# Pooled attention and a ReLU² feed-forward on one core: the exchange of q's halves on GpSimd or VectorE instead of by DMA

## The chip, the cores and the metric

The kernel runs on one core of a Trainium2 chip. The metric is the device time of one execution in microseconds; the kernel before was run three times. The core's engines are TensorE (PE; its weight loads are listed as PEld), VectorE (DVE), ScalarE (ACT), GpSimd (POOL) and SyncE (SP), which here only issues DMAs.

## The reference

Attention over four batches of eight heads, with the queries averaged in pairs, and then a feed-forward with a squared ReLU on the heads laid side by side:

```python
# q, k, v: (4, 8, 1152, 64) f32; w_in: (512, 2048); w_out: (2048, 512)
q_pool = q.reshape(B, H, S // 2, 2, D).mean(axis=3)          # 576 queries a head
scores = np.matmul(q_pool, k.transpose(0, 1, 3, 2)) / np.sqrt(D)
scores = scores - np.max(scores, axis=-1, keepdims=True)
attn = np.exp(scores)
attn = attn / (np.sum(attn, axis=-1, keepdims=True) + 1e-09)
x = np.matmul(attn, v)                     # -> (2304, 512) after a transpose
h = np.maximum(x @ w_in, 0.0)
out = (h * h) @ w_out
```

## The kernel before

**Tiling.** The 32 heads are worked through as 16 pairs of two heads. A pair has nine chunks of 128 queries by 1152 keys, so there are 144 chunks. Eight of them are of one head, and one holds the last 64 queries of both. Operands of matmuls are pairs of fp16 numbers, a high and a low part, whose products are added up; pairs 0 to 3 keep some operands in f32.

**A pair's preparation** (`prep(n)`, n is the number of the pair). SP loads k, q and v (LK, LQ, LV or LF). The two queries of a pair are added (QS, L486). A scale is found with a small matmul or sums of squares (GR, GM or QK, QQ, QV, then GF, GS, GE). q is scaled and split into a high and a low part (QA, L343 or L345; QD, L374), and so is k (KA, KD). A transposing DMA turns each of them: QT (L646) writes tile `qT`, KT (L633) writes tile `kT`. QT puts the high part of q on 64 partitions and the low part on the other 64. The low plane `qT[:, 1]` needs the halves the other way round, so step QX (two instructions, z = 0 and 1) copies each half of `qT[:, 0]` to the other 64 partitions. For pairs 1 to 4 (`'QXD': (1, 2, 3, 4)`) QX is a DMA from SBUF to SBUF, issued by SP at L652; for pairs 5 to 15 it is a copy on VectorE or GpSimd at L655. Pair 0 (`'FS': (0,)`) works in f32 and has no QX. A chunk's scores S wait for KT and both QX of their pair.

**A chunk.** S (L760, or L755 for the shared chunk), the maximum on VectorE (MX, L771), its bias (MB, L778 or L781), the exponential on ScalarE (EX, L795). For pairs 0 to 3 TensorE turns the result (TP, L836) and VectorE or ScalarE copies it to tile `PT` (TC, L846 and L848); for the other pairs it is split in two fp16 parts (HI, L799; LO, L807) and turned by a DMA (TR, L810). Two groups of matmuls per pair multiply with v (PV, L947 or L955).

**The feed-forward.** The result is worked on in nine blocks of 256 tokens (`block`). A block's columns are normalized (RV, RT, RB, XR: L1006 to L1046), scaled and split (XQ to XD), then there are eight steps of the hidden layer (H, L1119; HA, G1, G2, G3 square the ReLU) and eight of the output (O, L1168). Before that both weight matrices are loaded in sixteen parts (L1222) and turned into fp16 pairs (lines 1230 to 1347).

**The order.** Each operation is entered with `plan.add`: a name, the engines that may do it with a cost for each, what it depends on, and a position (`at`). `Plan.order` then simulates the engines, slots of buffers and a clock of TensorE, and writes out one program per engine. Among the operations that can start on an engine within its slack (`slPE` to `slSP`) it takes the one with the lowest priority number, which is the position plus an offset of the kind of operation (tables `off` and `off0`; `off0` counts up to the first block). An operation that may run on two engines goes to the one that can start it sooner, unless the other would end it earlier by more than `pen`. In the model a GpSimd operation waits for VectorE operations of the kinds in `LOCK`, QX among them, and these for it. Engines run their programs in order, so an instruction that waits holds all behind it.

The lines around the change:

```python
        def qx(o, z):
            t = qT(n).rearrange("p l c m -> p l (c m)")
            a, b_ = 64 * z, 64 - 64 * z
            if o["eng"] == "SP":
                nc.sync.dma_start(out=t[a : a + 64, 1], in_=t[b_ : b_ + 64, 0])
            else:
                e = nc.vector if o["eng"] == "DVE" else nc.gpsimd
                e.tensor_copy(t[a : a + 64, 1], t[b_ : b_ + 64, 0])
...
                add(("QX", n, z), {"SP": 850} if n in cfg("QXD", ()) else alt("QX", DVE=470, POOL=1500), [("QT", n)] + old, lambda o, z=z: qx(o, z), need)
```

## Time and profile before

| | before |
|---|---|
| median of 3 runs | 796.21 us (793.77 to 802.07) |
| profiled execution | 796.25 us |
| its span, first to last instruction | 794.4 us |
| TensorE busy | 743.8 us (94%) |
| VectorE busy | 571.4 us (72%) |
| ScalarE busy | 589.7 us (74%) |
| GpSimd busy | 350.1 us (44%) |
| chain that ended last: PE, DVE, ACT, DMA | 78%, 7%, 5%, 5% |

The busy shares are means over stages that differ: up to about 200 us the weights are prepared and pairs 0 to 4 begun; then scores, PV and the feed-forward share TensorE; from about 645 us on only the feed-forward is left. A wait of an engine is listed with what ended it. Idle time of an engine matters only where others wait for what it does next.

### The profile page before, as it was taken

How to read it: one execution, taken by the hardware profiler on the slowest of the kernel's cores; microseconds unless marked ns; L12 is line 12 of the kernel's file. 1: busy time of each engine (PE TensorE's matmuls, PEld its weight loads, DVE VectorE, ACT ScalarE, POOL GpSimd, SP SyncE). 2: the span in 40 equal slices, each digit the busy share in tenths (PEclk: the TensorE clock that was granted, in tenths of full speed). 3: DMA queues.
4: the chain of work that ended last, by engine and by line, in shares of the span. 5: the costliest groups of instructions: out<-in, count | busy, mean ns of one | idle time of the engine just before them, and what ended most of it. 6: DMA issues, size and time to landing. Idle time of an engine off the chain costs nothing.

```text
span 794.4 us, 15338 instructions
## 1 busy us (share of the span) xinstructions
PE 743.8 (94%) x5998; PEld 491.7 (62%) x5998; DVE 571.4 (72%) x920; ACT 589.7 (74%) x874; POOL 350.1 (44%) x240
## 2 busy tenths in 40 slices
PE   5889888888999999979999999999999999999997
PEld 4665555555766676546756775577567657785654
DVE  4789987787789798787879888898898764202311
ACT  5776967899798798688987997899989864403512
POOL 2455421346686475544646575575366321001200
PEclk8899899999899999979999999999999999999999
DMA  8686573417889999999999999999999991000011
GB/s 325 225 233 187 167 204 106 120 31 142 168 172 199 194 225 218 219 206 215 186 212 199 217 208 207 202 228 195 209 217 191 173 183 25 1 2 13 14 27 28
DMA packets 324840, 128.96 MB, mean 162 GB/s; under 512 B 307104, under 2 KB 307872, under 8 KB 324768
## 3 DMA queue, kind: packets, MB, share of 16 engines
q1 hardware_dynamic: 324768, 127.98, 77.3%
q8 instruction: 47, 0.77, 0.4%
q14 instruction: 25, 0.20, 0.1%
HBM read 45.09 MB, written 4.72 MB: 63 GB/s over the span
## 4 chain that ended last, share of the span: by engine, by line
PE 78%; DVE 7%; ACT 5%; DMA 5%; issue 3%; SPq 1%; POOL 0%; DVEq 0%; ACTq 0%; POOLq 0%
PE ba L1168 17%; PE ba L1119 17%; PE s L760 12%; PE ba L955 10%; PE bt L1168 7%; PE bt L1119 6%; DVE s L771 3%; PE ba L836 3%; DMA region<-in_moe_w_in_dram 2%; PE ba L947 2%; ACT buf L795 2%; PE s L755 2%; DMA w<-in_moe_w_out_dram 2%; DVE PT L848 1%; ACT PT L846 1%
## 5 line engine op out<-in xcount | busy, mean ns | idle before, releaser
L771 DVE TENSOR_SCALAR_CACHE_REDUCE s<-s,esc 128x1152 f32<-128x1152 f32 x135 | 190.9, 1420 | 32.2 <-PE s L760 21.9
L1119 PEld LDWEIGHTS <-w 128*128 128x128 f16 x1728 | 169.4, 99 | 33.1 <-issue 7.0
L795 ACT ACTIVATE buf<-s,ca 128x1152 f32<-128x1152 f32 x144 | 174.4, 1212 | 14.2 <-DVE s L771 7.7
L807 POOL TENSOR_TENSOR buf<-buf,buf 128x1152 f16<-128x1152 f32 x53 | 130.9, 2472 | 54.1 <-ACT buf L799 44.2
L760 PE MATMUL s<-kT,qT 128*128 128x512 f16 x720 | 137.6, 330 | 9.3 <-ACT buf L795 9.0
L1168 PE MATMUL ba<-w,region 128*128 128x512 f16 x624 | 142.2, 379 | 1.3 <-ACT region L1129 0.7
L1168 PEld LDWEIGHTS <-region 128*128 128x128 f16 x864 | 82.8, 98 | 96.3 <-issue 2.5
L1119 PE MATMUL ba<-region,w 128*128 128x256 f16 x1104 | 128.7, 275 | 1.3 <-DVE x L1046 1.2
L799 ACT ACTIVATE buf<-buf 128x1152 f16<-128x1152 f32 x107 | 124.5, 1163 | 5.9 <-DMA PT<-buf 1.7
L760 PEld LDWEIGHTS <-qT 128*128 128x128 f16 x720 | 63.6, 100 | 66.9 <-issue 18.1
L807 DVE TENSOR_TENSOR buf<-buf,buf 128x1152 f16<-128x1152 f32 x55 | 77.1, 1404 | 14.4 <-ACT buf L799 14.1
L955 PE MATMUL ba<-PT,v 128*64 128x320 f16 (+1 forms) x1296 | 85.4, 290 | 0.0
L955 PEld LDWEIGHTS <-v 128*64 128x64 f16 x1296 | 70.8, 111 | 14.7 <-issue 7.1
L1146 POOL TENSOR_TENSOR region<-region 128x512 f16<-128x512 f32 x35 | 49.2, 1405 | 51.4 <-ACT region L1139 50.0
L1146 DVE TENSOR_TENSOR region<-region 128x512 f16<-128x512 f32 x37 | 29.1, 793 | 58.7 <-ACT region L1139 55.8
L836 PE MATMUL ba<-ident,buf 128*128 128x128 f32 x324 | 54.4, 296 | 14.8 <-ACT buf L795 5.5
L1134 ACT ACTIVATE region<-region 128x512 f16<-128x512 f32 x72 | 45.1, 626 | 20.3 <-PE bt L1168 17.3
L836 PEld LDWEIGHTS ba<-ident,buf 128*128 128x128 f32 x324 | 36.4, 148 | 30.7 <-ACT PT L846 8.7
L1168 PE MATMUL bt<-w,region 128*128 128x512 f16 x240 | 52.6, 379 | 0.0
L1142 POOL TENSOR_TENSOR region<-region 128x512 f32<-128x512 f32 x11 | 14.6, 1329 | 83.6 <-ACT region L1134 83.6
L846 ACT ACTIVATE PT<-ba 128x384 f32<-128x384 f32 x76 | 35.7, 490 | 18.6 <-PE ba L836 17.1
L1119 PE MATMUL bt<-region,w 128*128 128x256 f16 x432 | 48.7, 273 | 0.0
(189 smaller groups left out, 944.1 us busy)
## 6 DMA issues: line engine op xcount, KB each, us to landing
raw<-in_q_dram SPq DMA_DIRECT2D x32, 288.0 KB, 3.8
raw<-in_k_dram SPq DMA_DIRECT2D x15, 576.0 KB, 4.8
region<-in_moe_w_in_dram SPq DMA_DIRECT2D x8, 1024.0 KB, 6.2
w<-in_moe_w_out_dram SPq DMA_DIRECT2D x8, 1024.0 KB, 5.8
raw<-in_v_dram SPq DMA_DIRECT2D x12, 576.0 KB, 4.7
out_dram<-buf SPq DMA_DIRECT2D x22, 128.0 KB, 2.4
v<-in_v_dram SPq DMA_DIRECT2D x4, 576.0 KB, 6.2
out_dram<-half SPq DMA_DIRECT2D x14, 128.0 KB, 3.3
```

Source lines behind the costliest of these rows:

```text
L760: nc.tensor.matmul(s[:, x, :w], lhsT=qt[:, l].rearrange("p c m -> p (c m)")[:, 128 * c0 + h : 128 * c0 + h + 255 : 2], rhs=rhs, **st)
L771: nc.vector.tensor_scalar(st3(), st3(), sc, 3e38, op0=ALU.mult, op1=ALU.min, accum_out=a[:, x : x + 1])
L795: nc.scalar.activation(P(), st3(), AF.Exp, bias=a[:, 1:2], scale=s1, accum_out=col)
L799: nc.scalar.activation(hl()[:, 0], P(), AF.Copy)
L807: e.tensor_tensor(out=hl()[:, 1], in0=P(), in1=hl()[:, 0], op=ALU.subtract)
L836: nc.tensor.matmul(t[:, y], lhsT=P()[:, c * 128 : (c + 1) * 128], rhs=ident, is_transpose=True, start=(y == 0), stop=(y == 2), skip_group_ ...
L846: nc.scalar.activation(out, t, AF.Copy)
L955: nc.tensor.matmul(px[h * 64 : (h + 1) * 64, 64 * r * (1 - h) : 64 * r * (1 - h) + N], lhsT=vv[:, h, kc, vl, :], rhs=p2(vi, r, h, 9 * pl + ...
L1119: nc.tensor.matmul(ph[:, f2], lhsT=w16[0][:, SLOT[f // 4], wl, a, f % 4 * 128 : (f % 4 + 1) * 128], rhs=xhl()[:, xl, a], start=(i == 0), s ...
L1134: nc.scalar.activation(gt[u][:, 0], rt[u % 2], AF.Square)
L1146: e.tensor_tensor(out=gt[u][:, 1], in0=rt[u % 2], in1=gt[u][:, 0], op=ALU.subtract)
L1168: nc.tensor.matmul(p[:, :DM], lhsT=g[:, gl, f % 2, tt * 128 : (tt + 1) * 128], rhs=w16[1][:, SLOT[f // 4], wl, f % 4], start=(f == 0 and g ...
```

## The change

`QXD` becomes empty, so the two QX of pairs 1 to 4 are no longer entered for SP but for VectorE or GpSimd, as those of pairs 5 to 15 are. All the numbers that steer the planner (positions of the weights, slacks, penalty and both tables of offsets, over two hundred in all) are replaced by others. No line of code differs otherwise. The diff, cut to single entries of the one line:

```diff
-CFG = {'SPLIT': 0, 'TURN': [], 'TURNB': [],
...
-'WSP': 0.4394, 'WOF': 23.2581, 'MSP': 10.7319, 'pen': 4650.4498, 'bl': 16.0216, 'slPE': 66.7964, 'slACT': 353.0356, 'slDVE': 0.0, 'slPOOL': 569.0059, 'slSP': 247.8544, 'off': {'ED': 1246.3547, 'EX': 5849.5041, 'G1': -389.0426,
...
-'PART': 1, 'QXD': (1, 2, 3, 4), 'MSC': (0, 1, 2, 3, 4, 5, 6, 7, 8, 9, 10, 11, 12, 13, 14, 15), 'FS': (0,), 'NSG': (12, 13, 14, 15)}
+CFG = {'SPLIT': 0, 'TURN': [], 'TURNB': [],
...
+'WSP': 0.0186, 'WOF': 22.3361, 'MSP': 10.3534, 'pen': 6673.337, 'bl': 12.9223, 'slPE': 128.2463, 'slACT': 204.4283, 'slDVE': 0.0, 'slPOOL': 713.7895, 'slSP': 699.821, 'off': {'ED': 1155.7513, 'EX': 5204.1755, 'G1': -68.3962,
...
+'PART': 1, 'QXD': (), 'MSC': (0, 1, 2, 3, 4, 5, 6, 7, 8, 9, 10, 11, 12, 13, 14, 15), 'FS': (0,), 'NSG': (12, 13, 14, 15)}
```

## Rows read from the trace of the kernel before

**Rows 1.** The page's head, and span and granted clock of the core.
```profile
span 794.4 us, 15338 instructions
...
core 0: 794.4 us, clock 0.973
```

**Rows 2.** Busy time by stretch: length, engines (instructions), granted clock, DMA share, GB/s.
```profile
0.00:199.30 199.30, 163.49 (x1261) 108.49 (x1262) 157.25 (x265) 156.79 (x235) 82.85 (x57) 0.95 0.60 174
199.30:340.00 140.70, 139.68 (x1153) 90.85 (x1154) 114.96 (x173) 115.49 (x171) 88.29 (x58) 0.98 1.05 198
340.00:366.00 26.00, 19.10 (x157) 11.47 (x153) 22.70 (x47) 22.62 (x33) 13.78 (x10) 0.79 1.09 217
366.00:645.00 279.00, 276.79 (x2369) 185.19 (x2369) 239.22 (x368) 244.10 (x359) 152.56 (x105) 0.99 1.08 203
645.00:794.40 149.40, 144.77 (x1072) 95.72 (x1066) 37.23 (x72) 50.66 (x80) 12.65 (x11) 0.99 0.13 28
```

**Rows 3.** TensorE around 350 us: start, length, operation, [idle before]; first a chain row.
```profile
313.21 3.79 PE ba L955 x54
...
341.04 1.14 PE L760 MATMUL s<-kT,qT 128*128 128x512 f16 x6 [0.82 <-ACT buf L795]
...
346.33 2.08 PE L760 MATMUL s<-kT,qT 128*128 128x512 f16 x6 [2.26 <-ACT buf L795]
...
350.18 2.08 PE L760 MATMUL s<-kT,qT 128*128 128x512 f16 x6 [1.55 <-ACT buf L795]
352.18 5.30 PE L955 MATMUL ba<-PT,v 128*64 128x320 f16 x54
...
359.38 2.78 PE L1119 MATMUL ba<-region,w 128*128 128x256 f16 x24
...
365.41 4.43 PE L1119 MATMUL ba<-region,w 128*128 128x256 f16 x24 [1.16 <-DVE x L1046]
```

**Rows 4.** End of the head: timeline, a chain row, and the stretch after it.
```profile
196.75 0.46 DVE L655 COPY qT<-qT 64x1152 f16<-64x1152 f16 x1 [2.12 <-DMA qT<-half]
...
199.31 2.08 PE L1119 MATMUL ba<-buf,w 128*128 128x256 f16 x9 [3.68 <-DVE region L1046]
...
199.31 5.28 PE ba L1119 x24
...
200.00:210.00 10.00, 10.00 (x69) 6.87 (x68) 6.19 (x10) 5.72 (x9) 5.33 (x5) 0.75 0.75 141
```

**Rows 5.** The exchange: DMAs by line (page), copies by line (busy, mean, idle before).
```profile
qT<-qT SPq DMA_DIRECT2D x8, 144.0 KB, 3.5
...
L655 POOL COPY qT<-qT 64x1152 f16<-64x1152 f16 x10 | 13.8, 1380 | 9.6 <-DMA qT<-half 7.1 <-DMA qT<-buf 2.2
...
L655 DVE COPY qT<-qT 64x1152 f16<-64x1152 f16 x12 | 12.1, 1005 | 3.5 <-DMA qT<-half 3.0 <-DMA qT<-buf 0.3
```

**Rows 6.** Timeline of SP's queue in the head, for pairs 1 and 3.
```profile
39.84 0.51 SPq L455 DMA_DIRECT2D raw<-in_k_dram  x1
42.23 1.16 SPq L652 DMA_DIRECT2D qT<-qT  x2
43.56 1.08 SPq L1222 DMA_DIRECT2D region<-in_moe_w_in_dram  x1
46.01 4.01 SPq L633 DMA_TRANSPOSE kT<-buf  x1
...
109.28 3.43 SPq L633 DMA_TRANSPOSE kT<-buf  x1
...
114.03 0.60 SPq L652 DMA_DIRECT2D qT<-qT  x1
```

**Rows 7.** Busy time from 110 to 120 us, columns as in rows 2.
```profile
110.00:120.00 10.00, 9.74 (x75) 6.04 (x72) 7.09 (x8) 6.32 (x14) 1.16 (x1) 1.00 0.97 261
```

**Rows 8.** Timeline of a pair's two copies, one on each engine.
```profile
356.06 1.21 POOL L655 COPY qT<-qT 64x1152 f16<-64x1152 f16 x1 [1.01 <-DMA qT<-buf]
356.30 1.28 DVE L655 COPY qT<-qT 64x1152 f16<-64x1152 f16 x1
```

More of the change, by code (lines that the diff above doesn't have):

```diff
@@ new lines @@
+CFG = {'SPLIT': 0, 'TURN': [], 'TURNB': [], 'WDP': ((1, 0), (1, 1), (1, 2), (1, 3)), 'WSP': 0.0186, 'WOF': 22.3361, 'MSP': 10.3534, 'pen': 6673.337, 'bl': 12.9223, 'slPE': 128.2463, 'slACT': 204.4283, 'slDVE': 0.0, 'slPOOL': 713.7895, 'slSP': 699.821, 'off': {'ED': 1155.7513, 'EX': 5204.1755, 'G1': -68.3962, 'G2': -123.9467, 'G3': 1333.2622, 'GE': 18.1176, 'GF': 26.104, 'GM': -745.2473, 'GR': -643.0342, 'GS': -84.6219, 'H': 954.7454, 'HA': -215.368, 'HI': -1269.3528, 'KA': 562.9266, 'KC': -57.49, 'KD': 497.1086, 'KT': -1299.5505, 'KX': 67.3497, 'LF': 35.8519, 'LK': -857.6213, 'LO': 760.731, 'LQ': 549.3415, 'LV': -11.1892, 'MB': -424.817, 'MX': 361.3027, 'O': 953.3253, 'OD': -275.6397, 'PV': 500.3755, 'QA': -1401.4099, 'QC': 29.2001, 'QD': 32.489, 'QK': 2138.8964, 'QQ': 146.18, 'QS': 2497.0738, 'QT': 1494.0203, 'QV': -11.834, 'QX': 1525.4262, 'QY': -276.7502, 'RB': 0.0, 'RT': 278.7151, 'RU': -195.812, 'RV': 249.435, 'S': 495.01, 'ST': 0.0, 'TC': -2615.772, 'TP': 409.8394, 'TR': 2599.4919, 'U0': -78.5472, 'U1': -57.609, 'U2': -4.104, 'U4': 39.0922, 'U5': -146.3559, 'UA': -84.0042, 'UB': 78.0938, 'UD': -134.7562, 'UG': 504.7818, 'UL': -415.8558, 'UM': 15.5013, 'US1': -635.3331, 'US2': -517.841, 'US3': -91.4049, 'VA': -109.6182, 'VD': -3.4512, 'W0': -284.5234, 'W1': -316.9133, 'W2': 2307.5158, 'W4': -13.01, 'W5': -32.0465, 'WA': -3.098, 'WD': 5824.783, 'WG': 373.7026, 'WL': 182.5255, 'WM': 231.0511, 'WS1': -78.0917, 'WS2': -2611.7598, 'WS3': 331.8007, 'XA': -778.7032, 'XD': -370.2665, 'XM': -210.263, 'XN': 63.9693, 'XO': 48.8333, 'XQ': 1.593, 'XR': -15.1029, 'XT': -199.6854, 'XU': -5.4353, 'XW': 57.8313, 'aG1': 215.9286, 'aG2': 181.1135, 'aG3': 3322.7748, 'aH': 524.2489, 'aHA': 315.5924, 'aO': 548.5746, 'aOD': -78.9785, 'aRB': 188.0562, 'aRT': 150.485, 'aRU': 36.8139, 'aRV': 455.1187, 'aST': -2.8218, 'aXA': 251.4545, 'aXD': 160.2636, 'aXM': 404.5088, 'aXN': -6.8193, 'aXO': 43.6287, 'aXQ': -286.9806, 'aXR': -104.2157, 'aXT': 0.0, 'aXU': -51.4745, 'aXW': 238.9049, 'zG1': -127.2733, 'zG2': 237.7114, 'zG3': 125.1926, 'zH': 62.4838, 'zHA': -114.0457, 'zO': -12.4775, 'zOD': -322.5224, 'zRB': 167.2084, 'zRT': 6.4244, 'zRU': -30.3756, 'zRV': 5.0063, 'zST': -706.033, 'zXA': 414.6013, 'zXD': 22.9561, 'zXM': -101.8686, 'zXN': -73.9566, 'zXO': 125.3875, 'zXQ': 1.9865, 'zXR': 314.746, 'zXT': -68.6324, 'zXU': 223.2691, 'zXW': -84.2701}, 'off0': {'ED': -320.0915, 'EX': 125.5949, 'G1': 248.867, 'G2': 110.9041, 'G3': -16.9689, 'GE': -47.3991, 'GF': -53.7139, 'GM': 404.5614, 'GR': 81.4246, 'GS': 386.4081, 'H': -53.165, 'HA': 321.1861, 'HI': 454.0458, 'KA': -73.3824, 'KC': 383.1779, 'KD': 32.3608, 'KT': -14.5959, 'KX': -109.4637, 'LF': -115.1952, 'LK': 283.9355, 'LO': -37.2674, 'LQ': -668.8801, 'LV': -6.9267, 'MB': 83.388, 'MX': 27.5904, 'O': -118.3342, 'OD': 608.16, 'PV': 109.2794, 'QA': 337.6865, 'QC': 336.4052, 'QD': -124.9362, 'QK': -273.3459, 'QQ': 129.9256, 'QS': 10.539, 'QT': -2000.7354, 'QV': 114.5733, 'QX': -194.2563, 'QY': -172.2764, 'RB': 96.2895, 'RT': 50.1838, 'RV': -16.9469, 'S': 0.6736, 'ST': -48.0614, 'TC': -136.814, 'TP': -1846.3967, 'TR': -590.0095, 'U0': 241.215, 'U1': 9.5267, 'U2': -333.3012, 'U4': 1.3978, 'U5': 166.1059, 'UA': 1.0166, 'UB': -165.2871, 'UD': -135.0975, 'UG': -341.5448, 'UL': -13.3372, 'UM': 163.4304, 'US1': 256.4171, 'US2': 1.0301, 'US3': 134.9024, 'VA': 140.927, 'VD': 568.9883, 'W0': 47.9826, 'W1': -423.8488, 'W2': 728.494, 'W4': -214.2481, 'W5': -106.9897, 'WA': -30.786, 'WD': -532.7241, 'WG': 117.0441, 'WL': -781.7529, 'WM': -460.7912, 'WS1': -0.4311, 'WS2': 84.5956, 'WS3': 173.9561, 'XA': 388.3773, 'XD': -123.6278, 'XM': 48.4282, 'XN': 62.3395, 'XO': -494.8718, 'XQ': -3.2534, 'XR': -12.8004, 'XT': 759.0058, 'XU': -0.293, 'XW': -0.2008, 'aG1': -470.7793, 'aG2': -105.6588, 'aG3': 379.2232, 'aH': 126.9171, 'aHA': 41.6135, 'aO': -179.083, 'aOD': -89.0891, 'aRB': 123.2573, 'aRT': -105.3376, 'aRU': 21.553, 'aRV': -75.9354, 'aST': -191.3426, 'aXA': -351.4751, 'aXD': -15.2288, 'aXM': -78.308, 'aXN': 382.8232, 'aXO': 10.5251, 'aXQ': 157.1809, 'aXR': 281.7874, 'aXT': -36.7704, 'aXU': 47.4239, 'aXW': -81.0074, 'zG1': -128.2889, 'zG2': 74.8859, 'zG3': -216.8134, 'zH': -687.1117, 'zHA': -13.0965, 'zO': 66.0008, 'zOD': 215.2758, 'zRB': -42.5762, 'zRT': -457.4963, 'zRU': -93.7426, 'zRV': -220.5694, 'zST': 3.3173, 'zXA': -48.9854, 'zXM': -20.2671, 'zXN': -180.6047, 'zXO': -90.0309, 'zXQ': 122.8555, 'zXR': -296.7451, 'zXT': -122.7678, 'zXU': 4.0233, 'zXW': -206.5981}, 'FV': (0, 1, 2, 3), 'PART': 1, 'QXD': (), 'MSC': (0, 1, 2, 3, 4, 5, 6, 7, 8, 9, 10, 11, 12, 13, 14, 15), 'FS': (0,), 'NSG': (12, 13, 14, 15)}
```

1 line of the change is left out of this document (removed).

## The prediction

> **What bounds the kernel now.** I first read the granted clock and the span, then the busy time by stretch, then the chain of waits, and last the timelines of the places that the change touches. The profiled execution took 796.25 us, of which 794.4 us are its span [rows 1]; the other 1.85 us lie around it. The median of the runs shown is 796.21 us, so the sums below, made against 796.25 us, can be read against the median as they stand.
>
> The table of stretches [rows 2] divides the span by what TensorE did. From 199.3 us on, TensorE is full: idle for 1.0 us of 140.7, 2.2 us of 279.0 and 4.6 us of the last 149.4. In these stretches the end moves only with TensorE's own work, and the change adds or removes no matmul. TensorE idles in two places. In the head (0 to 199.3 us) it idles 199.3 - 163.5 = 35.8 us in many small pieces, while VectorE is busy 157.3 us and ScalarE 156.8 us, each 79%; GpSimd is busy only 82.9 us and the DMA engines 60%. The head is a mesh of weight preparation and the first four pairs, in which no engine is full but VectorE and ScalarE are nearest to it. Between 340 and 366 us TensorE idles 26.0 - 19.1 = 6.9 us and its clock is 0.79 of the full rate: it had used up the feed-forward work of the blocks that were ready, and had only scores to do, each waiting for ScalarE's exponentials [rows 3]. So the span is TensorE's work plus about 50 us of idle time, 43 of them in those two places.
>
> The second place cost more than its idle time. After the gaps the clock fell from the upper level (2.4 GHz) to the lower (1.2 GHz): six score matmuls took 2.08 us twice in place of 1.14, a PV group of 54 matmuls 5.30 in place of 3.79, and 24 matmuls of a hidden layer 4.43 in place of 2.78 [rows 3]. That is 0.94 + 0.94 + 1.51 + 1.65 = 5.0 us, and with the idle time 11.9 us for one such stall. A smaller one ends the head: TensorE stands 3.68 us until 199.31, and its next 24 matmuls of the hidden layer, in a stretch with a clock of 0.75, take 5.28 us in place of 2.78 [rows 3, 4], so 3.7 + 2.5 = 6.2 us.
>
> **The change, part by part.** *Taken away:* eight DMAs of 144 KB, two for each of pairs 1 to 4, landing 3.5 us (median) after issue [rows 5]. Their place on SP's queue goes too, with the wait in it: for pair 1 the queue stood from 40.35 us until the transposed q had landed, issued two exchanges at 42.23, and only then the load of a weight part at 43.56 [rows 6]. This load is a link of the chain of waits. It could at best have been issued 43.56 - 40.35 = 3.2 us earlier; at worst nothing is gained, because its buffer was not free or the chain goes on by another link. I take 1.0 us, under the middle, since nothing here shows when the buffer came free.
>
> Is the exchange itself on the path? For pairs 1, 2 and 4 SP issues the exchange some us ahead of the transpose of k (pair 1: 42.23 against 46.01 [rows 6]), and the scores need both, so k is last. Only for pair 3 is the second half late: issued at 114.03, after k's transpose at 109.28 [rows 6]. But TensorE was busy 9.74 us of the 10 from 110 to 120 [rows 7], so a sooner pair 3 fills at most 0.26 us. I take 0.
>
> *Added:* eight copies of 64x1152, on whichever of VectorE and GpSimd the planner picks. The trace has 22 of the same form from pair 5 on: 12 on VectorE at 1.005 us, 10 on GpSimd at 1.380 us [rows 5]. In that ratio the eight are 4.4 on VectorE (4.4 us) and 3.6 on GpSimd (5.0 us). GpSimd has 199.3 - 82.9 = 116 us idle in the head, which hides its part. VectorE has 42 us idle, in pieces that mostly wait for TensorE, so some of the 4.4 us hides and some delays the maxima and splits that others wait for. Below, nothing; above, all eight on VectorE and all on the path, 8 x 1.005 = 8.0 us. I take a third of 4.4, 1.5 us, because VectorE is 79% busy but not the only engine on the path.
>
> A copy also holds whoever is behind it on its engine while it waits for q to land. VectorE did so for 3.5 us over its 12 copies, GpSimd for 9.6 us over its 10 [rows 5]; behind VectorE's copy stand the maxima, for which ScalarE waits, and then TensorE. The mean is 0.29 us a copy on VectorE, so 4.4 x 0.29 = 1.3 us; the old wait of SP's queue held loads instead. I take 0.3 us of this, since TensorE has a stall behind it in only one of the places seen; the dear end is a rival below.
>
> Last, the two engines can stand in each other's way. At 356.06 us GpSimd started such a copy (1.21 us); VectorE's twin began at 356.30 and took 1.28 us, where 0.46 us was enough at 196.75 [rows 4, 8]. It ended 0.31 us after GpSimd's. So one copy on GpSimd cost VectorE 0.82 us. Below, nothing; above, 3.6 x 1.38 = 5.0 us. The kernel's own planner already keeps copies and two-input operations of VectorE apart from GpSimd's in its model, so I take 0.2 us.
>
> The Trainium skill, "SBUF — State Buffer", section "Who interferes with whom", speaks against this change: VectorE and GpSimd contend for one pair of ports, which the one that starts first keeps for its whole instruction, while transfers by DMA use other ports. The pair at 356 us agrees with it. By that rule each GpSimd copy that meets such work of VectorE delays it in full: the 3.6 copies would cost up to 5.0 us in place of my 0.2, and the sum would be 802 us. With all eight on GpSimd it is the second rival below.
>
> *Found anew:* the whole order. All offsets, the slacks and the penalty differ, so each engine's program is another one from the first microseconds. Work on TensorE, the DMA bytes from and to DRAM, and the number of every other instruction stay as they are. What it is worth cannot be read from the trace of before; its scale can. The stall at 340 us is worth 11.9 us and the one at 199 us 6.2 us, and neither belongs to the algorithm: both are accidents of one order.
>
> The sum without the order: 796.25 - 1.0 + 0 + 1.5 + 0.3 + 0.2 = 797.25, **797 us**. For itself alone the exchange lies between -3.5 (3.2 + 0.26, nothing lost) and +8 us (all on VectorE).
>
> **The rivals.** *Faster, 784 us.* The new order leaves no block boundary bare: the stall of 340 to 366 us is gone, 796.25 - 11.9 = 784.4. For it: it is the only stall of its size after 200 us, TensorE has 149 us of pure feed-forward work left at the end [rows 2], so a few hidden layers held back would cover it. Against: such a boundary comes for each of the first blocks, and the order has to hit all of them.
>
> *Ports, 807 us.* All eight copies go to GpSimd, which idles most in the head, and each finds VectorE at work that it blocks, on the path: 8 x 1.38 = 11.0, 796.25 + 11.0 = 807.3. It decides from six copies on (8.3 us). For it: the pair at 356 us. Against: one blocked operation is not always one on the path.
>
> *A copy that waits at the head of VectorE's queue, 809 us.* At 196.75 us VectorE's copy had stood 2.12 us for the transposed q of pair 5; behind it stood the maxima and the multiplication for which TensorE then waited until 199.31 [rows 4]. One such stall cost 6.2 us with the low clock after it; two more among the eight give 796.25 + 12.4 = 808.7. It decides from two on. For it: 8 new copies at about the rate of the old. Against: in the head TensorE is not full, so part of such a stall falls into idle time that is there anyway.
>
> *One boundary more goes bare, 808 us.* The new order keeps the stall at 340 us and has another like it: 796.25 + 11.9 = 808.2.
>
> **How the numbers follow.** About 1% (8 us) is what a measurement of this kernel can tell from no change. Forecast (old idle time in new places, net effect of the copies small): 0.45, with a range of its own of 789 to 804. The faster rival: 0.28. Ports: 0.07; waiting copy: 0.11; a boundary more: 0.09. That gives faster by over 1% 0.28, within 1% 0.45, slower by over 1% 0.27. The predicted time is the forecast's, 797 us. The range has to reach into the faster rival (784, and 4 us below it if the stall at 199 us shrinks as well: 780) and into the slower ones (809, and some of the exchange's own bound: 813); that leaves about one in ten on each side.
>
> **What would show it.** In the profile after: no issue of q from q on SP, and 30 copies in place of 22, the eight new ones before about 170 us. The weight load behind pair 1's q goes out without standing behind the exchange. If the forecast is right, TensorE's idle time in the head stays at 33 to 40 us, VectorE's busy time there grows by some 4 us, and a stall of about 12 us is still found somewhere at the edge of two blocks. If the faster rival is right, TensorE's idle time after 200 us is under 4 us apart from the end. If ports: VectorE's two-input splits and copies grow longer on the mean, each beside a GpSimd copy. If the waiting copy: idle time before VectorE's new copies over 1 us, each followed by a gap on TensorE. The prediction is wrong in kind if TensorE's busy time changes by more than the clock explains, or if the head is longer or shorter by over 10 us.

## The result and the profile after

The changed kernel takes 805.67 us (median, 802.71 to 808.2), the kernel before 796.34 us beside it (793.72 to 803.6). The ratio is 1.0102 with a 95% interval of 1.0079 to 1.0125: slower by 8 us, between 6 and 10. That lies inside the predicted range, 9 us above the predicted time, and at the very edge of what I had called no change. The profiled execution of the kernel after is one of its longer ones (807.87 us), so the 11.5 us by which its span exceeds that of before are more than the 8 us of the ratio.

First the head of the page of the kernel after, and its busy time by stretch at the cuts of [rows 2], columns as there; the last but one row is the 40 us around 540 us, the last the 10 us of [rows 3].

```profile
span 805.9 us, 15316 instructions
...
core 0: 805.9 us, clock 0.982
```
```profile
0.00:199.30 199.30, 159.54 (x1233) 104.16 (x1235) 161.56 (x258) 151.57 (x232) 78.89 (x55) 0.97 0.52 158
199.30:340.00 140.70, 135.43 (x1154) 89.87 (x1150) 123.92 (x184) 118.70 (x179) 86.53 (x55) 1.00 1.07 203
340.00:366.00 26.00, 20.50 (x148) 11.50 (x146) 23.60 (x38) 17.40 (x27) 12.45 (x9) 0.87 1.05 214
366.00:645.00 279.00, 271.90 (x2320) 181.69 (x2318) 241.73 (x363) 239.39 (x356) 143.23 (x100) 0.99 1.06 200
645.00:805.90 160.90, 156.29 (x1157) 101.71 (x1153) 49.02 (x91) 59.21 (x92) 13.22 (x13) 0.99 0.20 40
...
520.00:560.00 40.00, 35.64 (x308) 25.79 (x307) 35.70 (x56) 34.53 (x53) 18.98 (x16) 0.96 1.05 193
...
350.00:360.00 10.00, 5.64 (x30) 2.93 (x32) 8.94 (x19) 6.33 (x10) 5.81 (x4) 0.67 0.93 199
```

TensorE's busy time adds up to 743.7 us, as before (163.49 + 139.68 + 19.10 + 276.79 + 144.77 = 743.8 [rows 2]). So the whole difference of the spans, 805.9 - 794.4 = 11.5 us, is TensorE standing idle. The cuts say where: in the head 39.8 us in place of 35.8, from 199.3 to 340 us 5.3 in place of 1.0, from 366 to 645 us 7.1 in place of 2.2, of which 4.4 fall between 520 and 560 us. The tail idles 4.6 us as before, and the bare block edge at 340 to 366 us is still there (5.5 in place of 6.9 us, clock 0.67 in its middle). VectorE is the engine that has more to do in each of the first two stretches: 161.6 in place of 157.3 us, and 123.9 in place of 115.0.

The copies and three groups of VectorE whose mean grew, by line (busy, mean ns | idle before), after:

```profile
L655 POOL COPY qT<-qT 64x1152 f16<-64x1152 f16 x15 | 21.7, 1449 | 19.4 <-DMA qT<-half 9.5 <-DMA qT<-buf 9.4
...
L655 DVE COPY qT<-qT 64x1152 f16<-64x1152 f16 x15 | 11.2, 746 | 1.1 <-DMA qT<-buf 0.8
...
L374 DVE SCALAR_TENSOR_TENSOR v<-raw,psc,v 128x576 f16<-128x576 f32 x24 | 32.2, 1345 | 0.8 <-ACT v L343 0.7
...
L486 DVE TENSOR_TENSOR raw<-raw 128x576 f32<-128x576 f32 x11 | 13.5, 1232 | 9.2 <-DMA raw<-in_q_dram 9.2
...
L1309 DVE TENSOR_SCALAR half<-ident,wm 128x128 f32<-128x128 f32 x2 | 2.5, 1242 | 0.1
```
and the same three groups before:
```profile
L374 DVE SCALAR_TENSOR_TENSOR v<-raw,psc,v 128x576 f16<-128x576 f32 x24 | 27.8, 1160 | 1.2 <-POOL v L345 1.1
...
L486 DVE TENSOR_TENSOR raw<-raw 128x576 f32<-128x576 f32 x8 | 6.6, 819 | 7.9 <-DMA raw<-in_q_dram 7.9
...
L1309 DVE TENSOR_SCALAR buf<-ident,wm 128x128 f32<-128x128 f32 x2 | 0.6, 286 | 0.1
```

Thirty copies stand where 22 stood [rows 5], 15 on each engine, and no DMA of q from q is left. The same instructions of VectorE became longer: 24 splits of v by 4.4 us, two tiny multiplications of 0.29 us by 1.9 us. An instruction of fixed size that takes longer was held up by something; the timelines further down show by what.

**A second yardstick.** The order is made by a planner that gives every operation a start. The 144 exponentials (L795) are the beat of the kernel, so I took the start of each from the trace and the planner's start of the same one, and call the difference lateness. It places a loss, to within a microsecond or so (the first chunks of runs with one and the same order differ by as much). Each run below is one execution, and executions of one kernel end up to 10 us apart (before: 793.72 to 803.6), so 2 or 3 us between two runs late in the table prove little by themselves. The planner's own end is 790.6 us for the order before and 792.9 for the order after: 2.3 us of the 11.5 are in the plan. The rest is lateness, which is, in us, for the kernels whose plan is one of these two (chunks are counted from 0; the names are those that stand behind the experiments' headings):

```
chunk        12     16     24     36     40     64     80    112    120    140
order of the kernel before
before     +0.6   -0.2   -0.1   -0.9   +3.3   +3.1   +4.6   +4.3   +4.4   +4.5
e1_split   +4.0   +3.3   +3.0   +4.2   +7.2   +6.5   +8.2   +8.5   +9.7   +9.3
e2_dve     -0.0   +0.4   +1.7   +2.2   +6.5   +6.7   +9.1   +9.4  +10.2   +9.9
e8_pool    +4.0   +3.7   +4.5   +5.0   +8.9   +8.5  +10.3  +10.3  +10.8  +10.5
e11_pair1  -0.6   -0.9   -0.3   +0.3   +4.6   +4.2   +8.2   +7.4   +8.5   +8.2
e6_wait    -0.0   -0.8   -0.6   -1.3   -0.1   +1.0   +2.0   +3.0   +3.1   +3.2
e12_soon   -0.2   -1.0   -0.9   -0.2   -0.2   -0.9   +1.8   +1.0   +1.9   +1.5
order of the kernel after
after      +0.7   +4.0   +5.8   +5.4   +5.0   +5.3   +9.2   +8.3  +13.3  +14.0
e3_sp      -0.1   +3.3   +3.6   +3.0   +2.6   +2.8   +8.2   +7.3   +8.3   +9.0
e7_port    +1.9   +1.8   +0.4   +0.1   -0.3   -0.4   +4.0   +3.2   +8.2   +9.6
e10_both   -0.5   -0.6   +3.8   +4.9   +4.5   +4.5   +4.7   +4.9   +5.9   +6.5
e13_late   -0.7   -0.8   -1.6   -1.8   -2.2   -1.3   +2.3   +1.0   +5.2   +6.4
```

The kernel before loses 4.2 us at one place, between chunks 36 and 40 (the end of the head, [rows 4]), and 1.5 near chunk 78. The kernel after loses 3.3 between chunks 12 and 16, 2 up to chunk 24, 4 between 64 and 80, and 5 between 112 and 120. The experiments go by these places, but for that between 64 and 80.

### The profile page after: what moved, and what is told of

It reads as the page before. It is cut to its first block, busy times and chain, and to the rows that moved or that the text cites. A ratio compares the mean times of both kernels' runs of the same rounds, so it can differ in the third digit from the quotient of the medians.

```text
span 805.9 us, 15316 instructions
## 1 busy us (share of the span) xinstructions
PE 743.7 (92%) x5998; PEld 488.9 (61%) x5998; DVE 599.8 (74%) x930; ACT 586.3 (73%) x882; POOL 334.3 (41%) x230
## 4 chain that ended last, share of the span: by engine, by line
PE 70%; DVE 11%; ACT 9%; issue 5%; DMA 2%; POOL 2%; SPq 1%; DVEq 0%; POOLq 0%; ACTq 0%
PE ba L1168 16%; PE ba L1119 14%; PE s L760 11%; PE ba L955 9%; PE bt L1119 6%; PE bt L1168 5%; DVE s L771 4%; ACT buf L795 3%; PE ba L947 3%; PE ba L836 2%; ACT PT L846 1%; PE s L755 1%; DMA region<-in_moe_w_in_dram 1%; PE s L739 1%; POOL w L1347 1%
## 5 line engine op out<-in xcount | busy, mean ns | idle before, releaser
L1119 PEld LDWEIGHTS <-w 128*128 128x128 f16 x1728 | 167.7, 98 | 28.2 <-issue 3.9
L795 ACT ACTIVATE buf<-s,ca 128x1152 f32<-128x1152 f32 x144 | 174.9, 1215 | 8.2 <-DVE s L771 3.1
L807 POOL TENSOR_TENSOR buf<-buf,buf 128x1152 f16<-128x1152 f32 x53 | 130.0, 2453 | 65.5 <-ACT buf L799 55.2
L1168 PE MATMUL ba<-w,region 128*128 128x512 f16 x672 | 154.4, 381 | 0.0
L1119 PE MATMUL ba<-region,w 128*128 128x256 f16 x1080 | 125.5, 273 | 0.8 <-DVE region L1046 0.6
L1146 POOL TENSOR_TENSOR region<-region 128x512 f16<-128x512 f32 x39 | 53.6, 1375 | 123.3 <-ACT region L1139 122.8
L807 DVE TENSOR_TENSOR buf<-buf,buf 128x1152 f16<-128x1152 f32 x55 | 79.4, 1443 | 19.9 <-ACT buf L799 17.5
L1146 DVE TENSOR_TENSOR region<-region 128x512 f16<-128x512 f32 x33 | 30.9, 937 | 36.9 <-ACT region L1139 36.5
L1119 PE MATMUL bt<-region,w 128*128 128x256 f16 x456 | 51.4, 273 | 0.0
L374 DVE SCALAR_TENSOR_TENSOR buf<-raw,psc,buf 128x576 f16<-128x576 f32 x36 | 47.4, 1330 | 0.9 <-POOL buf L345 0.9
L1139 ACT ACTIVATE region<-region 128x512 f32<-128x512 f32 x66 | 41.6, 630 | 2.0
```

The source lines that it names most:

```text
L374: nc.vector.scalar_tensor_tensor(out=o, in0=x, scalar=s, in1=h, op0=ALU.mult, op1=ALU.subtract)
L795: nc.scalar.activation(P(), st3(), AF.Exp, bias=a[:, 1:2], scale=s1, accum_out=col)
L807: e.tensor_tensor(out=hl()[:, 1], in0=P(), in1=hl()[:, 0], op=ALU.subtract)
L1119: nc.tensor.matmul(ph[:, f2], lhsT=w16[0][:, SLOT[f // 4], wl, a, f % 4 * 128 : (f % 4 + 1) * 128], rhs=xhl()[:, xl, a], start=(i == 0), s ...
L1146: e.tensor_tensor(out=gt[u][:, 1], in0=rt[u % 2], in1=gt[u][:, 0], op=ALU.subtract)
L1168: nc.tensor.matmul(p[:, :DM], lhsT=g[:, gl, f % 2, tt * 128 : (tt + 1) * 128], rhs=w16[1][:, SLOT[f // 4], wl, f % 4], start=(f == 0 and g ...
```

## The experiments

Ratios are to the kernel before, run on the same chip.

**The exchange alone, in the order of before, one copy of each pair on each engine.** (e1_split) This separates the copies from the new order: the order stays word for word, only the engine of eight entries changes.

```diff
     seq = plan.order(("EX", NSTEP - 1))
+    for o in seq:
+        if o["name"][0] == "QX" and 1 <= o["name"][1] <= 4:
+            o["eng"] = ("POOL", "DVE")[o["name"][2]]
```


> The order of the kernel before, held fixed; only the eight exchanges of pairs 1 to 4 leave SP's queue and stand at the same places of the order as copies, the first half on GpSimd and the second on VectorE, as most stand in the changed kernel. Theory A (the exchange itself costs nearly nothing, the new order is what costs): 795 to 799 us. Theory B (the copies cost what the changed kernel lost): 802 to 807 us, with longer operations of VectorE beside the copies or idle time of VectorE before its new copies.

Measured: 799.3 us, 1.003 [0.9994, 1.0066]. A small loss, not clear of nothing. Its lateness rises to +4.0 by chunk 12 already; why, the run after the next shows.

**The same, all eight on VectorE.** (e2_dve) The edit is that of the last run with `"DVE"` for all.

> As the run before, but all eight copies on VectorE: the upper bound of the exchange by itself. Theory A: 796 to 800 us, because 4 to 8 us more of VectorE's time fall partly into its idle time in the head. Theory B: 804 us or more.

Measured: 803.65 us, 1.007 [1.0035, 1.0104], so 2.8 to 8.3 us. My bound from above for VectorE's time was eight copies of 1.005 us, 8.0 us. The timeline of VectorE in the head shows how it gets there:

```profile
44.04 0.92 DVE L655 COPY qT<-qT 64x1152 f16<-64x1152 f16 x2
...
78.15 2.77 DVE L655 COPY qT<-qT 64x1152 f16<-64x1152 f16 x2
...
110.75 0.46 DVE L655 COPY qT<-qT 64x1152 f16<-64x1152 f16 x1
```
A copy by itself takes 0.46 us, half of the mean that I had used, since that mean contains blocked ones; of the eight only the second of the two from 78.15 us on was blocked (2.77 - 0.46 = 2.3 us), by GpSimd's weight operation L1264, which started at 78.27. All eight together, the four from 110.75 us on being alike, are 0.92 + 2.77 + 4 x 0.46 = 5.5 us of VectorE. By lateness the execution is 3.2 us behind the kernel before at chunk 40 (+6.5 against +3.3; the last copy starts at 151.83 us, chunk 40 at 209.6), and 5.4 us behind at the end (+9.9 against +4.5); the ratio is worth 5.6 us. So over half of VectorE's 5.5 us was not hidden. The 2.2 us that come after chunk 40 can't be put down to the copies by this one execution.

**All eight on GpSimd, in the order of before.** (e8_pool) `"POOL"` for all. This is the port rival in its purest form.

> The order of the kernel before, held fixed; all eight exchanges of pairs 1 to 4 on GpSimd, at the same places. The run with half of them on GpSimd took 799.3, with all on VectorE 803.7. Theory A (what costs is VectorE's time): 796 to 798 us, because GpSimd is idle for over half of the head. Theory B (a copy on GpSimd blocks VectorE for its length, on the path): 803 to 807 us.

Measured: 802.05 us, 1.0049 [1.003, 1.0068]: 2.4 to 5.4 us, not the 11 of the rival, and between the two theories. And over half of the loss does not lie where the copies are. It is there by chunk 12 (+4.0 against +0.6, where the end has +10.5 against +4.5), and comes in a place with no copy. Timelines of VectorE and GpSimd there, of before:

```profile
55.70 1.16 POOL L368 TENSOR_SCALAR region<-region 128x1024 f32<-128x1024 f32 x1 [0.16 <-DMA region<-in_moe_w_in_dram]
56.11 1.29 DVE L1239 TENSOR_SCALAR region<-w 128x1024 int16<-128x1024 int16 x1
57.33 1.21 DVE L1255 SCALAR_TENSOR_TENSOR region<-region 128x1024 int32<-128x1024 int32 x1
...
57.49 3.04 POOL L1264 TENSOR_TENSOR w<-w,region 128x1024 f32<-128x1024 f32 x1 [0.64 <-DVE region L1239]
```
and with the copies on GpSimd:
```profile
41.64 0.37 SPq L1222 DMA_DIRECT2D region<-in_moe_w_in_dram  x1
...
43.93 3.23 POOL L655 COPY qT<-qT 64x1152 f16<-64x1152 f16 x2
...
55.78 0.69 DVE L1239 TENSOR_SCALAR region<-w 128x1024 int16<-128x1024 int16 x1
56.13 1.29 POOL L368 TENSOR_SCALAR region<-region 128x1024 f32<-128x1024 f32 x1 [0.71 <-DMA region<-in_moe_w_in_dram]
57.40 2.12 POOL L1264 TENSOR_TENSOR w<-w,region 128x1024 f32<-128x1024 f32 x1
...
57.46 3.15 DVE L1255 SCALAR_TENSOR_TENSOR region<-region 128x1024 int32<-128x1024 int32 x1 [0.99 <-POOL region L368]
```
Before, VectorE started 0.16 us ahead, took 1.21 us, and GpSimd waited. Now GpSimd starts 0.06 us ahead, takes 2.12, and VectorE's operation takes 3.15: 1.9 us longer, after a wait of 0.99 us for GpSimd's operation in front of it, L368. It is there that the order turns. Before, L368 started 0.41 us ahead of VectorE's L1239, which took 1.29 us beside it, so GpSimd waited for L1239 and came second at 57.4 too; now L1239 starts 0.35 us ahead and takes 0.69, and GpSimd goes on without a wait.

One way in which the copies of pair 1, 12 us earlier, reach this place is in the trace. Beside them VectorE's split of k took 1.69 us (46.09 to 47.78; before, 0.81 us from 45.17), so SP issued the transpose of k at 47.80 in place of 46.01 [rows 6] and the weight load behind it at 50.64 in place of 50.13; L368 waits for this load and started 0.43 us later. L1239 started 0.33 us sooner; the trace does not show that this comes from the copies. What the copies hold up directly is not what is lost: at chunk 8 (52.5 us) the run is no later than before (+0.6 against +1.1). The Trainium skill, "SBUF — State Buffer", section "Who interferes with whom", says that whoever starts first keeps the shared pair of ports for its whole instruction; the two traces agree from both sides. The line at 41.64 also answers my term for SP's queue: the weight load goes out at 41.64 in place of 43.56 [rows 6], 1.9 us sooner, and the run is still late.

**Pair 1 on VectorE, pairs 2 to 4 on GpSimd.** (e11_pair1) If the turned start is the cause, this one keeps six of eight copies on GpSimd and should lose almost nothing.

```diff
+            o["eng"] = "DVE" if o["name"][1] == 1 else "POOL"
```


> The order of the kernel before, held fixed; the exchange of pair 1 on VectorE, those of pairs 2 to 4 on GpSimd. With all eight on GpSimd (802.05 us) GpSimd's weight operation at 57.4 us started 0.06 us ahead of VectorE's, which was then blocked (3.15 us where 1.21 is usual); in the kernel before VectorE's started 0.16 us ahead. Theory (the loss comes from this one meeting, brought about by pair 1's copies in GpSimd's queue): no lateness of the exponentials at 75 us, and 797 to 799 us. Rival (each copy on GpSimd costs its share): 800 to 802 us.

Measured: 798.69 us, 1.0017 [0.9994, 1.0039]. The order of starts is that of before again (L368 0.16 us ahead of L1239), and lateness at chunk 12 is -0.6:

```profile
56.09 1.21 DVE L1255 SCALAR_TENSOR_TENSOR region<-region 128x1024 int32<-128x1024 int32 x1
...
56.25 3.05 POOL L1264 TENSOR_TENSOR w<-w,region 128x1024 f32<-128x1024 f32 x1 [0.64 <-DVE region L1239]
```
So six copies on GpSimd and two on VectorE cost 1.4 us, at most 3.1, where my sum for the port rival had 8.3 for the six. (The profiled execution loses 2 us more than before between chunks 64 and 80; as the median lies lower, that is not in every execution.) What costs here is less a copy's own block than a neighbour's start turned round.

The traces agree on this start. L368 is ahead of L1239 by 0.41, 0.06 and 0.15 us in the three executions whose order is that of before up to there (before, e6_wait, e12_soon), by 0.34 and 0.16 with pair 1 on VectorE (e2_dve, e11_pair1), and behind by 0.01 with one copy on each engine (e1_split) and by 0.35 with both on GpSimd (e8_pool). Only in the last two does L1255 take 3.15 us, and only they have +4.0 at chunk 12. As the three without a change differ by 0.35 us among themselves, a kernel with the gap near zero may fall to either side from one execution to the next. The executions of e1_split, from 794.6 to 805.03 us, would fit that; it is not shown.

**The new order with the DMAs back.** (e3_sp) The opposite cut: the order of the kernel after stays, the eight exchanges go to SP.

> The order of the changed kernel, held fixed; only the eight copies go back to SP's queue as DMAs, at the same places of the order. Theory A: 803 to 808 us, the loss stays because it is the order's. Theory B: 795 to 799 us, the loss is gone. A little more than the changed kernel (up to 3 us) is possible, because in this order SP's queue has other transfers behind the exchange.

Measured: 801.15 us, 1.0052 [1.0019, 1.0085]. That is between the two theories. So the new order alone costs about 4 us (1.5 to 6.8), the copies in it about another 4 (1.0102 against 1.0052). These last seem to be only in part the copies' own time: in the two profiled executions the kernel after is 2.4 us behind this one at chunk 36, 1.0 at chunk 112 and 5.0 at chunk 120, far behind the last copy.

**The small operation at 69.9 us.** (e7_port) The kernel after loses its first 3.3 us here. Timelines of GpSimd and VectorE, and the wait of TensorE at the end:

```profile
69.87 2.14 POOL L1264 TENSOR_TENSOR w<-w,region 128x1024 f32<-128x1024 f32 x1 [4.30 <-DVE wm L1307]
...
69.70 0.15 DVE L1307 TENSOR_REDUCE wm<-wsc 128x1 f32<-128x4 f32 x1
69.89 2.20 DVE L1309 TENSOR_SCALAR half<-ident,wm 128x128 f32<-128x128 f32 x1
...
74.04 4.07 DVE L374 SCALAR_TENSOR_TENSOR buf<-raw,psc,buf 128x576 f16<-128x576 f32 x3
...
78.36 0.55 PE L836 MATMUL ba<-ident,buf 128*128 128x128 f32 x3 [1.11 <-DVE wm L1319]
```
GpSimd starts 0.02 us after the small reduction at 69.70, which the profile names as its releaser (VectorE's weight operation L1255 ends just ahead of it). VectorE's next, by itself 0.29 us long, is 0.02 us behind GpSimd and takes 2.20 us, as long as GpSimd's. The planner's model sees nothing there: WS1, the step to which the small product belongs, is not among the kinds in `LOCK`, and the plan has it side by side with GpSimd's operation. The kernel that tests this puts the two small ones (WS1) ahead of the weight operation:

```diff
+    names = [o["name"] for o in seq]
+    x = names.index(("WS1", 0))
+    y = max(i for i in range(x) if seq[i]["eng"] == "DVE")
...
+    seq.insert(y, seq.pop(x))
```


> The order of the changed kernel; only one small operation of VectorE (the 128x128 product at L1309 with the maximum ahead of it) is put ahead of the weight operation that stood before it, so that it runs before GpSimd's L1264 is released, not together with it. In the changed kernel it took 2.20 us there, 0.29 us elsewhere. Theory (VectorE and GpSimd blocking each other is what makes the new order later than planned): the exponentials from about 75 us on come 1.9 us sooner or more, and the time is 802 to 804 us. Rival (the head has slack at that place, or another operation is blocked in its stead): 805 to 806 us.

Measured: 801.18 us, 1.0053 [1.003, 1.0075]: moving 0.44 us of work by one place in one queue gave back half of the whole loss, more than I had expected. The timeline of VectorE and GpSimd there:

```profile
70.08 0.29 DVE L1309 TENSOR_SCALAR half<-ident,wm 128x128 f32<-128x128 f32 x1
70.28 1.22 DVE L1255 SCALAR_TENSOR_TENSOR w<-w 128x1024 int32<-128x1024 int32 x1
...
71.58 2.14 POOL L1264 TENSOR_TENSOR w<-w,region 128x1024 f32<-128x1024 f32 x1 [4.81 <-DVE ba L599]
...
73.44 2.39 DVE L374 SCALAR_TENSOR_TENSOR buf<-raw,psc,buf 128x576 f16<-128x576 f32 x3
```
The three splits behind it also fell from 4.07 to 2.39 us, because they no longer lie beside GpSimd's next two operations of 1.22 and 1.50 us. Lateness at chunk 24 is +0.4 in place of +5.8.

**Both repairs together.** (e10_both)

> The order of the changed kernel with both edits that gave back 4.5 us each: the eight exchanges on SP's queue as DMAs, and the small product at L1309 ahead of the weight operation. Theory (the exchange on the engines and the engines blocking each other in the new order are two causes that add up): 805.7 - 4.5 - 4.5 = 796 to 799 us, about the kernel before. Rival (both edits remove one and the same lateness of VectorE in the head): 800 to 802 us, as each of them alone.

Measured: 800.51 us, 1.0048 [1.0023, 1.0072]: not 4 + 4 us, but as much as either alone. The waits of TensorE name the reason:

```profile
PE s L760 <- DMA qT<-qT: 2.7, 1, 2.7
```
With the block gone, the scores of pair 2 come sooner in the new order, and then the DMA exchange is late: TensorE stands 2.7 us at 88.8 us for it, with a clock of 0.83 from 84 to 94 us, and lateness rises from -0.6 to +3.8 by chunk 24. In the trace of before no wait of TensorE on that DMA exists. In the run with the DMAs alone TensorE waits 1.4 us for them. So whether the exchange is on the path hangs on the order. With the small operation moved, copies and DMAs come out alike (801.18 and 800.51 us).

**What the search is worth.** (e4_replan, e9_replan2) Each exchange with the numbers of the other kernel: the planner plans anew, with no new search. The edit of the first is shown; the second makes the reverse one in the kernel after.

```diff
-CFG = {... 'QXD': (1, 2, 3, 4), ...}
+CFG = {... 'QXD': (), ...}
```


> All numbers of the kernel before, only QXD is empty, so that the planner makes another order with numbers that were not found for it. The planner's own end is 810.8 us where it was 790.6 for the kernel before and 792.9 for the changed one. If the chip follows the planner's order as closely as it did for these two (3.8 and 13.0 us more in the span): a measured time of 816 to 826 us. A rival: the planner's figure means little, and the time is 795 to 808 us, like both others.

> All numbers of the changed kernel, but QXD as before (exchanges of pairs 1 to 4 by DMA), and the planner makes the order with them. Its own end is 815.2 us, where it is 792.9 for the changed kernel. If the chip follows the plan: 820 to 830 us. If DMA were better by itself whatever the numbers: below 805 us.

Measured: 817.91 us, 1.0238 [1.0188, 1.0287], for the numbers of before with copies; 820.19 us, 1.0278 [1.0259, 1.0297], for the numbers of after with DMAs. The planner says 810.8 and 815.2 us for them, against 790.6 and 792.9 for the two kernels: the chip follows the plan. The planner's numbers fit one choice of engines: with the other, some 19 us are lost in the one case and 14 in the other. A comparison of two choices under one set of numbers would have said little about the choice.

**The waiting copy at the end of the head.** (e6_wait, e12_soon) The dearest rival rested on one place: VectorE stands 2.12 us for pair 5's transposed q at 196.75 [rows 4], which I had priced at 6.2 us. Here the two copies of pair 5 go later in the queues, nothing else changes.

```diff
+    late = [o for o in seq if o["name"][:2] == ("QX", 5)]
+    seq = [o for o in seq if o not in late]
+    y = next(i for i, o in enumerate(seq) if plan.start[plan.at[o["name"]]] >= 206000)
+    seq[y:y] = late
```


> The order of the kernel before; only the two copies of pair 5's exchange move some 10 us later in the order (behind what was planned up to 206 us; the pair's first scores come at about 224 us), so that VectorE no longer stands at the head of its queue until q has landed while the normalization of the first block waits behind it. Theory (one copy that waits there costs TensorE 3.7 us and the lower clock after it another 2.5): 3 to 6 us less than before, 790 to 793 us. Rival (the stall only moves to what is late next): within 1 us of the kernel before.

Measured: 795.54 us, 0.9974 [0.9954, 0.9995]: 2 us, not 6. Lateness at chunk 40 is gone (-0.1), but comes back to +1.0 and later +3. TensorE's wait at the end of the head fell to 1.47 us, yet its 24 matmuls behind it still took 4.45 us. At its new place VectorE's copy met GpSimd again:

```profile
205.62 2.37 POOL L807 TENSOR_TENSOR buf<-buf,buf 128x1152 f16<-128x1152 f32 x1 [0.63 <-POOL ca L781]
...
205.99 2.32 DVE L655 COPY qT<-qT 64x1152 f16<-64x1152 f16 x1
```
So the same was tried some 5 us earlier, where the timeline of GpSimd has a gap (`>= 201200` for `>= 206000`).

> The order of the kernel before; only the two copies of pair 5's q, at which VectorE and GpSimd stood 2.1 and 2.9 us at the end of the head, are put some 4 us later in their queues (planned start past 201.2 us), instead of some 10 us later as in the run before that moved them. There GpSimd is free by the timeline of before (nothing from 202.6 to 206.6 us), so its copy does not lie beside the subtraction that blocked VectorE's for 1.9 us in the run with 10 us. Theory (the standing of VectorE at the transposed q cost the lateness of 4 us at the end of the head, and the run with 10 us gave 2.2 us of it back through that blocking): 793 to 795 us, ratio 0.994 to 0.998, and lateness of the exponentials of under 1 us at chunks 40 to 43. Rival (lateness in a stretch where TensorE is full is absorbed whatever its size): 795.5 to 797 us, as with 10 us or as before.

Measured: 793.43 us, 0.9948 [0.9922, 0.9974]: 4.1 us faster than before, between 2.1 and 6.2, and faster than both kernels. VectorE, GpSimd, TensorE, and the stretch after it, to be held against [rows 4]:

```profile
202.35 0.45 DVE L655 COPY qT<-qT 64x1152 f16<-64x1152 f16 x1
...
199.97 1.14 POOL L655 COPY qT<-qT 64x1152 f16<-64x1152 f16 x1
...
197.78 2.78 PE L1119 MATMUL ba<-buf,w 128*128 128x256 f16 x24 [1.47 <-DVE region L1046]
...
200.00:210.00 10.00, 9.51 (x86) 7.07 (x85) 9.04 (x18) 9.34 (x14) 7.22 (x5) 1.00 1.00 209
```
TensorE waits 1.47 us in place of 3.68, its next 24 matmuls take 2.78 us in place of 5.28, and the clock is 1.00 in place of 0.75: both halves of my price are there, 2.2 + 2.5 = 4.7 us. The second half does not follow from the first alone, since the run with 10 us had the same wait and still lost 1.7 of the 2.5 us. Not all of it stays: by lateness 3.5 us are saved at chunk 40 and 3.0 at the end. The intervals of the two runs overlap, so that the shorter move is the better one is likely, not shown.

**The place at 540 us.** (e13_late) The kernel after loses another 5 us between chunks 112 and 120. Timelines of GpSimd and VectorE at its start:

```profile
535.56 1.54 POOL L1146 TENSOR_TENSOR region<-region 128x512 f16<-128x512 f32 x1
537.18 3.37 POOL L807 TENSOR_TENSOR buf<-buf,buf 128x1152 f16<-128x1152 f32 x1
...
536.01 2.31 DVE L807 TENSOR_TENSOR buf<-buf,buf 128x1152 f16<-128x1152 f32 x1
538.24 2.92 DVE L374 SCALAR_TENSOR_TENSOR v<-raw,psc,v 128x576 f16<-128x576 f32 x1
```
About 1.35 and 0.82 us are usual for VectorE's two. The run was to take GpSimd's two away, on top of the moved small operation:

```diff
+    for o in seq:
+        if o["name"] in (("G3", 4, 4), ("LO", 116)):
+            o["eng"] = "DVE"
```

> The changed kernel's order with the small weight-scale operation moved ahead (801.2 us in that run), and in addition two operations near 531 to 541 us, GpSimd's subtraction of a hidden layer (L1146, 1.54 us) and of an exponential (L807, 3.37 us), given to VectorE, so that nothing of GpSimd lies beside VectorE's L807 and L374 there (2.31 and 2.92 us, in place of 1.35 and 0.82). Theory (the lateness of 4 to 5 us at chunks 115 to 120 comes from these blocked operations): lateness there falls by 2 us or more and the time is 798 to 800 us, ratio about 1.002. Rival (VectorE's own time, now 2 us more there, or ScalarE sets it): lateness unchanged within 1 us, 800.5 to 802 us.

Measured: 801.3 us, 1.0055 [1.0024, 1.0086], no change against 801.18 (1.0053). But I had aimed past the place. I had found the two operations by the planner's times, without the 8 us by which the kernel was late there, and so moved to VectorE the two of the same kind that come 6 us and more behind. The pair that I meant is still blocked (2.31 and 2.93 us, at 528.69 and 530.92), and VectorE has 2 us more to do.

What the runs of the same order show without an edit says more. From chunk 114 to 115 lateness rises by 1.3 to 1.4 us in all five of them, and all five hold the blocked pair. At chunk 117 it rises by 2.7 in the kernel after and in the run with the moved operation, and not at all in the two with DMAs. What differs there is VectorE's L486 (the two queries of a pair added), which waits for a load of q. Timelines of VectorE, GpSimd, ScalarE and TensorE, of the kernel after:

```profile
548.94 2.39 DVE L486 TENSOR_TENSOR raw<-raw 128x576 f32<-128x576 f32 x1 [1.14 <-DMA raw<-in_q_dram]
...
548.34 2.38 POOL L807 TENSOR_TENSOR buf<-buf,buf 128x1152 f16<-128x1152 f32 x1 [3.70 <-ACT buf L799]
...
551.36 0.68 ACT L578 ACTIVATE half<-raw 128x576 bf16<-128x576 f32 x1 [1.92 <-DVE raw L486]
...
552.19 0.38 PE L591 MATMUL ba<-acc,cols 128*128 128x2 f32 x2 [1.38 <-ACT half L578]
```
and of the same order with DMAs, VectorE and GpSimd:
```profile
546.81 0.76 DVE L486 TENSOR_TENSOR raw<-raw 128x576 f32<-128x576 f32 x1
...
547.37 2.43 POOL L807 TENSOR_TENSOR buf<-buf,buf 128x1152 f16<-128x1152 f32 x1 [3.70 <-ACT buf L799]
```
With DMAs VectorE starts 0.56 us ahead and takes 0.76 us; in the kernel after it starts 0.60 us behind and takes 2.39, ScalarE waits 1.92 us for it and TensorE 1.38 us for ScalarE. It is the turned start once more, almost 400 us behind the last copy that the change added (153.55 us). Even the run that missed agrees on the one part that it did touch: it took this GpSimd operation away, its L486 takes 0.76 us, and its rise at chunk 117 is 1.9 in place of 2.7, now with ScalarE waiting for the busier VectorE. That L486 alone makes the 2.7 us is thus a comparison of runs, not an experiment on it.

The same comparison fits half of the loss between chunks 64 and 80, at which no run was aimed. From chunk 64 to 65 lateness rises by 2.0 to 2.1 us in the three runs of this order with copies, and in each L486 starts behind GpSimd's L807 and takes 2.1 to 2.5 us (in the kernel after 309.89 against 309.00, 2.10 us). In the two with DMAs it starts ahead (in the run with both repairs 308.09 against 308.18), takes 0.76 us, and lateness does not rise.

## Why the prediction held, and where it did not

**What bounds the kernel** was read rightly: TensorE's busy time stayed, the clock hardly moved (0.982 against 0.973 [rows 1]), and all 11.5 us of the profile are idle time of TensorE. What I said to look for came: 30 copies, the eight new ones before 170 us (45 to 154 us), 39.8 us idle in the head (33 to 40 foretold), VectorE's busy time there up by 4.3 (4 foretold), the bare block edge still there. The head is not longer: chunk 40 starts at 205.8 us in place of 206.4. The faster rival needed that edge gone and fell; so did one more bare edge. Of the waiting copy there is nothing: VectorE's 15 copies waited 1.1 us in all. The sign for the ports came by half: the splits of v grew, but of the 12 that took over 1.0 us two lay beside a GpSimd copy, neither of them a new one, and nine beside GpSimd's L807.

**The term for SP's queue, -1.0,** came to nothing. The load did go out 1.9 us sooner (41.64 for 43.56) but no run with it is ahead at chunk 12 by more than the microsecond that executions of one order differ by. The bound "at worst nothing" was the value.

**The exchange off the path, 0,** was right for the order of before and wrong as a property of the exchange: in the new order the DMA is waited for, 1.4 us in all, and 2.7 us in one piece with the small operation moved.

**VectorE's time, +1.5,** was the term that failed in size, in two ways that went against each other. The unblocked copy is 0.46 us, not 1.005; but I let two thirds of it be hidden, and with all eight on VectorE (5.5 us) 3.2 us had come out by chunk 40 and 5.6 [2.8, 8.3] at the end. "VectorE is 79% busy but not the only engine on the path" was no reason for a third: 79% is a mean over the whole head and says nothing of the places where others wait for VectorE.

**Ports, +0.2, and "GpSimd's idle 116 us hides its part"** is the step that failed in kind. I counted a block as the length of one copy lying on one operation, and took little of it because the planner's model keeps such operations apart. The copies themselves cost little, as the run with six of them on GpSimd shows (+1.4 us, at most 3.1). But each entry shifts what stands behind it in the queues, and where operations of the two engines start within some tenths of a microsecond of each other a start can turn round, and costs 2 us and what follows. The model is no guard against that: it does not list the small product of 0.29 us at all, and the pair at 57.4 us, which it does list, it plans 0.16 us apart, less than executions differ. Idle time of an engine hides the duration of its work, not the shift of its other work. The pure port rival had 807 us for all eight on GpSimd, which measured 802.05, and by another mechanism than the copies' own blocks. By the rule of the Trainium skill ("SBUF — State Buffer", section "Who interferes with whom"), as I had used it, each copy that meets VectorE delays it in full, and the sum came to an estimate of 802 us with 3.6 copies on GpSimd; that this is near 802.05 is chance. The rule agrees with the traces, and I had applied it to the wrong operations.

**A copy that waits, +0.3, and its price of 6.2.** The price was worked out rightly piece by piece (2.2 + 2.5 of 3.7 + 2.5 came back) and was high as an end-to-end price: 4.1 us [2.1, 6.2], since some wait remains and some of the gain is lost later.

**The order found anew** I had put at no sign. Planned, the new order with its copies is 2.3 us worse; run, it is 8. The difference is in good part blocks of this kind: the moved small operation alone is 3.9 us of it (1.0102 against 1.0053).

So the sum, 797 us, was low by 9 us, outside the forecast's own range of 789 to 804. That 805.67 us lies within 780 to 813 is luck as far as the mechanism goes: the range reached so far up for copies that wait, a second bare edge and the bound of the exchange, and neither of the first two came. Of the measured 8 us some 4 belong to the new order with its turned starts and some 4 to the copies in it, and the two can't be added up freely, as the run with both repairs shows. What stays open: the losses between chunks 64 and 80 (4 us, where before had 1.5) and at chunk 117, for which there are only the comparisons above, and the other half of the first, for which there is nothing.

## What to carry to other kernels

When a small operation goes to another engine, do not price it by its duration over that engine's idle time: look at which neighbours in that queue move, and whether one of them, on VectorE or GpSimd, starts within some tenths of a microsecond of an operation of the other; in the places seen here, who was first decided over some 2 us. Put short operations that others wait for ahead of the instruction that releases the other engine, not behind it. And compare an exchange with the order frozen and with the order searched anew, for they are two changes; lateness against one's own plan shows where each loses.

## What the runs showed of the hardware

- The same pair of operations of VectorE and GpSimd takes 1.21 and 3.04 us when VectorE starts 0.16 us ahead, and 3.15 and 2.12 us when GpSimd starts 0.06 us ahead. By themselves they take 1.21 and 2.13 us, so the later one loses nearly all that is left of the earlier one.
- A small size does not save the later one: a 128x128 multiplication of 0.29 us, started 0.02 us behind a GpSimd operation of 2.14 us, took 2.20 us.
- A copy of 64x1152 fp16 takes VectorE 0.46 us and GpSimd 1.14 us when neither meets the other; the means of 1.005 and 1.380 us that I had read contain the blocks.
